# Routing and expert loads moved between two DMA queues in a fused attention and mixture-of-experts kernel

## The chip, the cores and the metric

One core of a Trainium2 chip runs the kernel. The metric is the device time of a run in microseconds (us). The core has five engines that run side by side, each through its own list of instructions in order: PE (matmuls), DVE (vector operations), ACT (activations, casts and copies), POOL (slow elementwise work, gathers) and SP (which only issues DMAs). DMAs are issued by SP, ACT or POOL and carried out by 16 shared DMA engines.

## The reference

Three layers follow each other. Attention: 2 batches, 8 heads, 576 positions, 64 wide; four heads see the last 32 positions, four see every 32nd position. Its result x is 1152 tokens of 512 numbers. A first mixture of 8 experts, of which each token uses one:

```
logits = x @ w_gate + modality_bias[modality_id]
e_idx = np.argmax(logits, axis=1)
...
for e in range(E):
    mask = e_idx == e
    h = np.maximum(x[mask] @ w1[e], 0.0)
    out[mask] = gate_w[mask, None] * (h @ w2[e])
```

And a second mixture of 4 experts, which every token uses, weighted by `domain_probs`. Each expert's first layer is 512 x 1024 and its second 1024 x 512, all in fp32.

## The kernel before

**Attention.** The 20 units of attention run in software steps s = 0 to 24 (L711 to L750): step s computes the scores of unit s (L307 to L341), the softmax of unit s and the result rows of unit s - 4 (`norm`, L350), the product with V of unit s - 3 (L398) and the transposes of the result of unit s - 5 (`xtr`, L425, PE line L430, into one PSUM bank that ACT copies out, L432 and L438). SP loads Q, K and V in pieces (`load_str`, `load_loc`, L197 to L223), small tables between the last of them (L237 to L245: constants, gate weights, bias, modalities, domain probabilities), and writes each unit's result rows to DRAM (L378, L383), from which tiles of tokens are gathered later.

**Routing.** `logits_part` (L442) multiplies transposed results with the gate weights (L450); `logits` (L458) transposes the sums (L466) and finds each token's expert; `ranks` (L511) and `lanes` (L524) number the tokens of each expert; L842 is the matmul that yields the list of tokens of every tile, `idx16`. The first batch is routed while the second is still in attention (`route0`, L668). Its favourite expert gets a tile of its own, the fill tile (`plain_tile`, L609: gather L596, transposes L617, first layer L623, transposes L636, second layer L643, scaled result L652), which runs in plain fp32 between the steps of the second batch's routing. SP reads the favourite from `gtab` (L165) and loads that expert's weights as eight blocks of 512 KB into `raws[0]` to `raws[7]`: two in `route0`, the rest in steps from 20 on. `EF` says how many pieces of the fill tile follow each step.

**Overflow tiles.** Behind the routing stands a nest of five branches on the number of tiles (L911), which is not entered. On its skip path SP waits until all transfers that it issued have landed; POOL does the same for its own.

**First mixture.** Eleven tiles of 128 tokens follow (`moe1`, L1005). Each fp32 operand is split into a high part (cast on ACT) and a rest (subtraction on DVE): `split`, L844, lines L846 and L847, for weights (`Weights.ahead`, at most `RING` = 10 blocks ahead), tokens (`x_parts`, transposes on PE L860) and hidden values (`htr`, L1032). The first layer is L1025, 24 matmuls for a tile; the second is L1046 to L1048. Weight blocks are loaded into the same eight `raws`, on the condition that the expert differs from that of the tile before. A transposed tile lies in one of two `ps_a` banks, which come free when the split is done.

**Second mixture.** 32 units of two blocks (L1257 to L1319, L1410 to L1430), not touched by the change.

The order on each engine is the order in which the program is written. Engines wait for each other by semaphores.

Of the kernel before, what the change touches and what calls it, by code (L numbers as in the profile page):

```python
# [18 lines left out]
ET = mybir.EngineType  # L19

P = 128
B, H, S, D = 2, 8, 576, 64
STRIDE = 32
P = 128
NTOK = B * S
DM = H * D
E1, E2 = 8, 4
FF = 1024
KC = DM // P
FC = FF // P  # L30
# [81 lines left out]
def fused_kernel(  # L112
# [42 lines left out]
    def w1_block(e, c):  # L155
        return w1a[bass.ds(e, 1), c * P : (c + 1) * P, :].rearrange("o p f -> p o f")

    def w2_block(e, u):
        return w2a[bass.ds(e, 1), u * 256 : (u + 1) * 256, :].rearrange("o (i p) f -> p (o i) f", p=P)

    def load_block(raw, src, cond=None):
        nc.sync.dma_start(out=raw.rearrange("p (c f) -> p c f", c=src.shape[1]), in_=src, cond=cond)

    def expert_value(ap):
        return nc.values_load(  # L165
            ap,
            engines=[ET.SP],
            min_val=0,
            max_val=E1 - 1,
            skip_runtime_bounds_check_because="clipped on chip",  # L170
        )
# [64 lines left out]
    load_str(3, (nc.gpsimd, nc.gpsimd))()  # L236
    nc.sync.dma_start(out=ct, in_=cst)  # L237
    wgs = ap.tile([P, KC, 32], F32, name="wgs")
    bsb = ap.tile([P, 2, E1], F32, name="bsb")
    mdi = ap.tile([P, NTT], I64, name="mdi")  # L240
    dps = ap.tile([P, NTT, E2], F32, name="dps")
    nc.sync.dma_start(out=wgs, in_=wg.rearrange("(c p) e -> p c e", p=P))
    nc.sync.dma_start(out=bsb, in_=bias.rearrange("(o m) e -> o m e", o=1).to_broadcast([P, 2, E1]))
    nc.sync.dma_start(out=mdi[:TQ], in_=mod)
    nc.sync.dma_start(out=dps[:TQ], in_=dp.rearrange("(j p) e -> p j e", p=TQ))  # L245
    load_loc(2, nc.gpsimd)

    mk16 = ap.tile([P, MW], BF16, name="mk16")
# [419 lines left out]
    def route0():  # L668
        logits_part(0, 1)
        logits_part(0, 0)  # L670
        yield from logits(0)
        rk = ranks(0)
        fav = favourite(rk[:, TPB])
        for _ in range(4):
            next(fav)
        eg.append(expert_value(gtab[0:1, 0:1]))
        for c in range(W1A):
            load_block(raws[c], w1_block(eg[0], c))
        yield
        for n, _ in enumerate(turns(lanes(0, rk), fav)):  # L680
            if n % 2:
                yield
        yield from first_tile()
# [22 lines left out]

    W1A, W1S = 2, 20
    nw = W1A
    r0 = route0()
    EF = 0, 0, 1, 1, 1, 2, 4  # L710
    for s in range(NU + 5):  # L711
# [20 lines left out]
        if s == 12:  # L732
            late_setup()
        if s == NU - 1:
            for t in range(NST + 1, NSX + 1):
                nc.sync.dma_start(out=ye[t * P : (t + 1) * P, :], in_=zero[:, :XW])
# [4 lines left out]
        if s == NU:  # L741
            for _ in r0:
                pass
            logits_part(1, 1)
        if s >= W1S and W1A <= nw < FC:
            for _ in range(2 if s==W1S else 1):
                load_block(raws[nw], w1_block(eg[0], nw) if nw < KC else w2_block(eg[0], nw - KC))
                nw += 1
        if s > NU:
            early(EF[s - NU - 1])  # L750
    while nw < FC:
        load_block(raws[nw], w2_block(eg[0], nw - KC))
        nw += 1
    logits_part(1, 0)
# [250 lines left out]
    def moe1(mp, tiles, W, gs, pool, mid, after, before_last):  # L1005
# [3 lines left out]
        def xprep(k):  # L1009
            g = gs.pop(k)  # L1010
            y = mp.tile([P, XW], F32, name="y", bufs=3)
            with_rows(y, idx16[:, tiles[k] : tiles[k] + 1])
            xs[k] = x_parts(g) if k else x0
            ys[k] = y
            if k + 2 < n:
                gs[k + 2] = m1_gather(tiles[k + 2], pool)
# [35 lines left out]
        xprep(1)  # L1052
        W.ahead()
        for k in range(n + 1):
# [6 lines left out]
            if k > 0:  # L1061
                htr(k - 1, 0, ht)
            W.ahead()
            if k == n:
# [3 lines left out]
            if k > 0:  # L1068
                htr(k - 1, 1, ht)
            W.ahead()  # L1070
            if k < n:
                mm1(k, ph, 2)
                if 0 < k < n - 1:
                    xprep(k + 1)
                W.ahead()
                mm1(k, ph, 3)
                h = mp.tile([P, FF], F32, name="h")
                for i in range(2):
                    nc.scalar.activation(h[:, 512 * i : 512 * (i + 1)], ph[i], AF.Relu)
                hs[k] = h  # L1080
                W.ahead()
# [292 lines left out]
    PC = Pieces()  # L1374
    W.ahead(3)
    x0 = x_parts(gs[0], x0)
    W.ahead(4)
    for _ in fill:
        pass
    W.owner[KC:] = [None] * (RAW - KC)  # L1380
    W.load()
    W.ahead()
    ectx.close()
# [114 lines left out]
def lay_out(inp):  # L1498
# [40 lines left out]
    for o, n in STRS:  # L1539
# [5 lines left out]
    vstr = with_one(vstr.reshape(2, 2, NCT, GQ, D).transpose(3, 1, 0, 2, 4))  # L1545
    w_gate = np.asarray(inp["moe_w_gate"])

    w1b = np.asarray(inp["moe2_w1"]).reshape(E2, 2, 2, P, 2, FC // 2, P)
# [8 lines left out]
        "mod": np.asarray(inp["moe_modality_id"]).reshape(NTT, TQ).T,  # L1557
        "wg": np.concatenate([w_gate, np.zeros((DM, 32 - E1), w_gate.dtype)], axis=1),
        "bias": inp["moe_modality_bias"],
        "w1a": inp["moe_w1"],  # L1560
        "w2a": inp["moe_w2"],
        "dp": inp["moe2_domain_probs"],
        "w1b": w1b.reshape(E2, FC // 2, P, -1),
# [33 lines left out]
```

## Time and profile before

| | |
|---|---|
| Median of 3 runs (lowest, highest) | 632.52 us (631.8, 635.23) |
| The profiled execution: time, and span in the profile | 631.46, 629.7 us |
| PE busy | 596.2 us, 95% of the span |
| DVE, ACT, POOL busy | 417.2 us (66%), 350.7 us (56%), 249.5 us (40%) |
| Moved by DMA | 79.14 MB, mean 126 GB/s |

The profile's times count from the start of the span, which lies 1.76 us inside the execution's own time. PE and PEld are the matmuls and the weight loads of the same engine. The attention ends near 66 us, the fill tile near 91, the first mixture near 240, and the second takes the rest.

### The profile page before, as it was taken

What the parts mean: (1) busy time and instruction counts of PE and PEld (TensorE: products, weight loads), DVE (VectorE), ACT (ScalarE), POOL (GpSimd) and SP (SyncE); (2) the same over time, 40 slices, a digit from 0 to 9 for tenths busy, and PEclk for the clock granted to TensorE, in tenths of its full rate; (3) what the DMA queues carried; (4) which work ended last, traced back from release to release, by engine and by line L of the source; (5) the groups of instructions that cost most, each with busy time, mean ns of one, the idle gap of its engine ahead of it and who ended that gap; (6) DMA issues with size and microseconds to landing.
All of it is one profiled execution on the core that took longest, in us unless ns stands there. A gap on an engine that the chain in (4) does not pass through costs nothing.

```text
span 629.7 us, 10388 instructions
## 1 busy us (share of the span) xinstructions
PE 596.2 (95%) x3620; PEld 498.8 (79%) x3620; DVE 417.2 (66%) x738; ACT 350.7 (56%) x690; POOL 249.5 (40%) x309
## 2 busy tenths in 40 slices
PE   4897798999999989999999999999999999999995
PEld 3554446888877878888988889898889988999984
DVE  3467369999896875668677677575565567557541
ACT  2354169888988874555656555554444544444420
POOL 9312023113696444275657656332342112312203
PEclk9999799999998999999999999999999999999999
DMA  8983951543479764353223231322421223121002
GB/s 189 200 187 109 315 161 47 168 143 94 144 229 316 231 222 150 122 165 101 101 92 110 72 129 68 135 84 88 144 87 67 69 74 124 71 68 68 0 2 84
DMA packets 35346, 79.14 MB, mean 126 GB/s; under 512 B 6520, under 2 KB 9856, under 8 KB 34904
## 3 DMA queue, kind: packets, MB, share of 16 engines
q1 hardware_dynamic: 30632, 67.08, 33.8%
q0 software_dynamic: 2784, 7.95, 4.1%
q10 hardware_dynamic: 1872, 3.39, 1.4%
q8 instruction: 30, 0.49, 0.3%
q14 instruction: 28, 0.23, 0.1%
HBM read 98.49 MB, written 9.28 MB: 171 GB/s over the span
## 4 chain that ended last, share of the span: by engine, by line
PE 77%; ACT 2%; DVE 2%; issue 2%; DMA 2%; POOL 1%; SPq 0%; POOLq 0%; DVEq 0%; ACTq 0%
PE ps_b L1269 9%; PE ps_b L1270 9%; PE ps_b L1271 9%; PE ps_b L1025 8%; PE ps_b L1418 7%; PE ps_b L1417 7%; PE ps_b L1420 7%; PE ps_a L1417 3%; PE ps_a L1418 3%; PE ps_a L1420 3%; PE ps_b L1048 3%; PE ps_b L1047 2%; PE ps_b L1046 2%; PE ps_a L1032 1%; ACT wh L846 1%
## 5 line engine op out<-in xcount | busy, mean ns | idle before, releaser
L1189 DVE TENSOR_TENSOR wl<-raw,wh 128x512 fp32r<-128x512 f32 (+1 forms) x160 | 125.6, 786 | 51.7 <-ACT wh L1188 51.0
L847 DVE TENSOR_TENSOR wl<-raw,wh 128x1024 fp32r<-128x1024 f32 x88 | 107.5, 1252 | 20.0 <-ACT wh L846 19.6
L1188 ACT CAST wh<-raw 128x512 fp32r<-128x512 f32 (+1 forms) x160 | 102.9, 664 | 3.5 <-POOL raw L1212 3.3
L1209 POOL TENSOR_TENSOR raw<-raw 128x256 f32<-128x256 f32 x32 | 24.1, 753 | 200.1 <-DVE wl L1189 200.1
L846 ACT CAST wh<-raw 128x1024 fp32r<-128x1024 f32 x88 | 90.1, 1055 | 8.6 <-ACT y L1092 3.6
L1281 DVE TENSOR_TENSOR m2t<-ps_b,raw 128x320 f32<-128x320 f32 (+1 forms) x93 | 42.1, 453 | 40.3 <-PE ps_b L1271 39.2
L1269 PE MATMUL ps_b<-xh,wh 128*128 128x256 f32 x224 | 63.8, 285 | 1.0 <-DVE xh L1281 0.5
L1271 PE MATMUL ps_b<-xh,wl 128*128 128x256 f32 x224 | 63.0, 281 | 0.0
L1270 PE MATMUL ps_b<-xl,wh 128*128 128x256 f32 x224 | 63.0, 281 | 0.0
L1269 PE MATMUL ps_b<-x,wh 128*128 128x320 f32 x160 | 49.6, 310 | 0.0
L1270 PE MATMUL ps_b<-x,wh 128*128 128x320 f32 x160 | 49.4, 309 | 0.0
L1271 PE MATMUL ps_b<-x,wl 128*128 128x320 f32 x160 | 49.4, 309 | 0.0
L1269 PEld LDWEIGHTS ps_b<-xh,wh 128*128 128x128 f32 x224 | 42.2, 189 | 7.1 <-ACT raw L1302 0.9
L1270 PEld LDWEIGHTS ps_b<-xl,wh 128*128 128x128 f32 x224 | 42.2, 188 | 4.2
L1284 ACT ACTIVATE hh2b<-m2t 128x256 fp32r<-128x256 f32 (+1 forms) x45 | 20.0, 443 | 44.3 <-DVE m2t L1281 41.0
L1284 ACT ACTIVATE hh2a<-m2t 128x256 fp32r<-128x256 f32 (+1 forms) x42 | 18.7, 445 | 44.5 <-DVE m2t L1281 44.5
L1271 PEld LDWEIGHTS ps_b<-xh,wl 128*128 128x128 f32 x224 | 42.3, 189 | 0.0
L605 POOL DMA_INDIRECT y<-xx,idx x11 | 12.9, 1177 | 60.4 <-DMA ye<-y 41.3
L1046 PE MATMUL ps_b<-wh,hh 128*128 128x512 f32 x88 | 35.1, 399 | 1.5 <-ACT hh L846 1.5
L1417 PE MATMUL ps_b<-wh,hh2a 128*128 128x512 f32 x90 | 35.5, 395 | 0.0
L1418 PE MATMUL ps_b<-wl,hh2a 128*128 128x512 f32 x90 | 35.5, 395 | 0.0
L1417 PE MATMUL ps_b<-wh,hh2b 128*128 128x512 f32 x90 | 35.5, 394 | 0.0
(274 smaller groups left out, 1546.0 us busy)
## 6 DMA issues: line engine op xcount, KB each, us to landing
raw<-in_w1a_dram SPq DMA_DIRECT2D x48, 512.0 KB
raw<-in_w2a_dram SPq DMA_DIRECT2D x48, 512.0 KB
raw<-in_w1b_dram SPq DMA_DIRECT2D x32, 512.0 KB
raw<-in_w2b_dram SPq DMA_DIRECT2D x32, 512.0 KB
ye<-y ACTq DMA_DIRECT2D x11, 260.0 KB
kvl<-in_kvl_dram SPq DMA_DIRECT2D x2, 792.0 KB
ye<-he SPq DMA_DIRECT2D x5, 260.0 KB
kvl<-in_kvl_dram SPq DMA_DIRECT2D x2, 614.0 KB
```

What stands on the lines that cost most here:

```text
L846: nc.scalar.copy(dst_h, src)
L847: nc.vector.tensor_tensor(dst_l, src, dst_h.bitcast(F32), op=ALU.subtract)
L1025: nc.tensor.matmul(ph[i], xx[:, s], ww[:, 512 * i : 512 * (i + 1)], start=first, stop=last)
L1046: nc.tensor.matmul(py, hh[:, s], wh[:, f], start=(kc == 0), stop=False)
L1188: return (lambda: nc.scalar.copy(h[:, s], src[:, s])), (lambda: nc.vector.tensor_tensor(l[:, s], src[:, s], h[:, s].bitcast(F32), op=ALU.s ...
L1189: lambda: nc.vector.tensor_tensor(l[:, s], src[:, s], h[:, s].bitcast(F32), op=ALU.subtract)
L1269: nc.tensor.matmul(ph, wh[:, kc], xh, start=first and kc == 0, stop=False, skip_group_check=True)
L1270: nc.tensor.matmul(ph, wh[:, kc], xl, start=False, stop=False, skip_group_check=True)
L1271: nc.tensor.matmul(ph, wl[:, kc], xh, start=False, stop=kc == 1, skip_group_check=True)
L1417: nc.tensor.matmul(po, hh, wh, start=(fb == 0 and fh == 1), stop=False, skip_group_check=part)
L1418: nc.tensor.matmul(po, hh, wl, start=False, stop=False, skip_group_check=part)
L1420: nc.tensor.matmul(po, hl, wh, start=False, stop=last, skip_group_check=part)
```

## The change

POOL instead of SP issues the tables, and all eight blocks of the fill expert's weights, in one run at step 20, when POOL has read the favourite for itself. Two tables are laid out on the host so that each partition's part is one run. SP writes the zero rows (an area that later gathers may touch) at step 14 instead of step 19. The fill tile's transposes come only after the logits of the second batch, and its first layer is shared out otherwise (`EF`). The second tile's tokens are split among the first weight splits instead of after ten of them, and most of the calls of `W.ahead` in the round of the first tile go. The lines of the changed program are 6 or 7 lower from `late_setup` on: L841 there is L847 here, L854 is L860, L1073 is L1079.

```
     load_str(3, (nc.gpsimd, nc.gpsimd))()
-    nc.sync.dma_start(out=ct, in_=cst)
...
-    nc.sync.dma_start(out=wgs, in_=wg.rearrange("(c p) e -> p c e", p=P))
-    nc.sync.dma_start(out=bsb, in_=bias.rearrange(...))
-    nc.sync.dma_start(out=mdi[:TQ], in_=mod)
-    nc.sync.dma_start(out=dps[:TQ], in_=dp.rearrange("(j p) e -> p j e", p=TQ))
     load_loc(2, nc.gpsimd)
+    nc.gpsimd.dma_start(out=ct, in_=cst)
+    nc.gpsimd.dma_start(out=wgs.rearrange("p c e -> p (c e)"), in_=wg)
+    nc.gpsimd.dma_start(out=bsb, in_=bias.rearrange(...))
+    nc.gpsimd.dma_start(out=mdi[:TQ], in_=mod)
+    nc.gpsimd.dma_start(out=dps[:TQ].rearrange("p j e -> p (j e)"), in_=dp)
...
         eg.append(expert_value(gtab[0:1, 0:1]))
-        for c in range(W1A):
-            load_block(raws[c], w1_block(eg[0], c))
...
-    W1A, W1S = 2, 20
-    nw = W1A
+    ZS = 14
-    EF = 0, 0, 1, 1, 1, 2, 4
+    EF = 0, 0, 0, 0, 0, 1, 3
...
-        if s == NU - 1:
+        if s == ZS:
             for t in range(NST + 1, NSX + 1):
                 nc.sync.dma_start(out=ye[t * P : (t + 1) * P, :], in_=zero[:, :XW])
...
-        if s >= W1S and W1A <= nw < FC:
-            for _ in range(2 if s==W1S else 1):
-                load_block(raws[nw], w1_block(eg[0], nw) if nw < KC else w2_block(eg[0], nw - KC))
-                nw += 1
+        if s == NU:
+            ep0 = expert_value(gtab[0:1, 0:1], ET.Pool)
+            for n in range(FC):
+                load_block(raws[n], w1_block(ep0, n) if n < KC else w2_block(ep0, n - KC), eng=nc.gpsimd)
...
         xprep(0)
         xprep(1)
-        W.ahead()
         for k in range(n + 1):
...
             if k > 0:
                 htr(k - 1, 0, ht)
-            W.ahead()
+                W.ahead()
...
             if k > 0:
                 htr(k - 1, 1, ht)
-            W.ahead()
+                W.ahead()
             if k < n:
                 mm1(k, ph, 2)
                 if 0 < k < n - 1:
                     xprep(k + 1)
-                W.ahead()
+                if k:
+                    W.ahead()
...
-    W.ahead(3)
-    x0 = x_parts(gs[0], x0)
-    W.ahead(4)
+    W.ahead(2)
+    x01 = [x_parts(gs[0], x0)]
+    W.ahead(KC + 1)
+    x01.append(x_parts(gs[1]))
+    W.ahead(KC + 2)
     for _ in fill:
         pass
     W.owner[KC:] = [None] * (RAW - KC)
     W.load()
-    W.ahead()
+    W.ahead(RING - 1)
```

POOL's order at the end of the attention, where the fill tile's gather (L596) and the gather of its routing rows (L605) stood next to each other (`raw_76` to `raw_83` are `raws[0]` to `raws[7]`; each ISA row works out a block's address):

```order
 L596 DMA g<-xe,idxe 128x512
+L165 TENSOR_LOAD gtab
+L162 ISA
+L162 DMA raw_76<-in_w1a_dram 128x1024
+L162 ISA
+L162 DMA raw_77<-in_w1a_dram 128x1024
+L162 ISA
+L162 DMA raw_78<-in_w1a_dram 128x1024
+L162 ISA
+L162 DMA raw_79<-in_w1a_dram 128x1024
+L162 ISA
+L162 DMA raw_80<-in_w2a_dram 128x2x512
```

Eight blocks (three more pairs of rows follow) now stand between L596 and L605, and ahead of the first tiles' gathers.

PE's order in the same place, from the last units' transposes to the ranks of the second batch (`ps_s` is the fill tile's first layer, `ps_m` logits and ranks):

```order
-L430 MATMUL ps_x<-mk,rw 128x128 x4
+L407 MATMUL ps_a<-kvl_157,pts 32x130 x8
+L430 MATMUL ps_x<-mk,rw 128x128 x6
+L450 MATMUL ps_m<-xtl,wgs 32x192 x6
 L617 MATMUL ps_t<-mk,g 128x128 x4
-L430 MATMUL ps_x<-mk,rw 128x128 x2
-L450 MATMUL ps_m<-xtl,wgs 32x192 x6
-L623 MATMUL ps_s<-raw_76,xte 128x512
 L466 MATMUL ps_m<-mk,lg 96x96 x2
-L623 MATMUL ps_s<-raw_76,xte 128x512
-L623 MATMUL ps_s<-raw_77,xte 128x512
+L623 MATMUL ps_s<-raw_76,xte 128x512 x2
```

The last transposes and the logits moved ahead of L617, and two of the eight matmuls of the fill tile's first layer instead of three now precede the ranks.

ACT's order in the round of the first tile, before (`h` is the first tile's hidden layer, `hh` its split, `xh` the second tile's tokens):

```order
L846 CAST wh<-raw_81 128x1024
L846 CAST xh<-ps_a 128x512
L846 CAST wh<-raw_82 128x1024
L846 CAST wh<-raw_83 128x1024
L846 CAST wh<-raw_76 128x1024
L1079 ACTIVATE h<-ps_b 128x512 x2
L846 CAST wh<-raw_77 128x1024
L846 CAST hh<-ps_a 128x512
```

And in the changed program:

```order
L840 CAST wh<-raw_80 128x1024
L1073 ACTIVATE h<-ps_b 128x512 x2
L840 CAST wh<-raw_81 128x1024
L840 CAST wh<-raw_82 128x1024
L840 CAST wh<-raw_83 128x1024
L840 CAST wh<-raw_76 128x1024
L840 CAST wh<-raw_77 128x1024
L840 CAST hh<-ps_a 128x512
```

Between `h` and `hh` stood one cast of weights, and now five; the second tile's `xh` moved up, ahead of the sixth weight cast. DVE's subtractions stand in the same order as these casts.

## Rows read from the trace of the kernel before

**Rows 1.** Windows: from and to, length, each engine's busy us, clock, DMA share, GB/s.
```profile
20.00:30.00 10.00, 7.88 (x95) 4.75 (x91) 4.16 (x16) 3.97 (x13) 1.51 (x3) 1.00 0.98 203
...
60.00:80.00 20.00, 15.43 (x108) 8.13 (x108) 8.81 (x55) 3.61 (x11) 2.73 (x3) 0.83 0.85 286
80.00:100.00 20.00, 17.58 (x75) 10.26 (x73) 14.05 (x21) 15.63 (x20) 9.30 (x8) 1.00 0.40 124
...
110.00:120.00 10.00, 10.00 (x52) 8.21 (x51) 9.28 (x10) 8.73 (x12) 2.18 (x2) 1.00 0.42 131
```

**Rows 2.** PE's timeline in the attention: start, us, instruction, idle before and releaser.
```profile
28.55 0.64 PE L323 MATMUL ps_s<-kvl,ql 128*32 128x128 f32 x16 [2.12 <-DMA ql<-in_qlo_dram]
...
49.20 0.64 PE L323 MATMUL ps_s<-kvl,ql 128*32 128x128 f32 x16 [1.03 <-DMA ql<-in_qlo_dram]
```

**Rows 3.** PE's timeline, fill tile and first tiles, and one later wait.
```profile
65.66 0.44 PE L430 MATMUL ps_x<-mk,rw 128*128 128x128 f32 x2 [0.46 <-ACT xtl L432]
68.86 1.12 PE L617 MATMUL ps_t<-mk,g 128*128 128x128 f32 x4 [2.76 <-DMA g<-xe,idxe]
...
70.33 2.08 PE L450 MATMUL ps_m<-xtl,wgs 128*32 128x192 f32 x12
...
74.21 0.52 PE L466 MATMUL ps_m<-mk,lg 96*96 96x96 f32 x2
...
76.66 4.54 PE L623 MATMUL ps_s<-raw,xte 128*128 128x512 f32 x10
81.03 0.45 PE L842 MATMUL ps_x<-boh,aoh 96*128 96x16 f16 x12
...
82.66 3.70 PE L643 MATMUL ps_a<-raw,hte 128*128 128x512 f32 x8
...
91.53 0.66 PE L860 MATMUL ps_a<-mk,g 128*128 128x128 f32 x4 [1.30 <-DVE xl L847]
91.94 0.71 PE L1025 MATMUL ps_b<-wh,xh 128*128 128x512 f32 x2
...
105.45 0.66 PE L860 MATMUL ps_a<-mk,g 128*128 128x128 f32 x4 [0.22 <-DVE hl L847]
...
107.33 0.40 PE L1046 MATMUL ps_b<-wh,hh 128*128 128x512 f32 x1
...
189.68 0.66 PE L1136 MATMUL ps_b<-mk,g 128*128 128x128 f32 x4 [2.29 <-DMA g<-ye,cidx]
```

**Rows 4.** Windows of 2 us, columns as in rows 1: clock, DMA share and rate.
```profile
68.00:70.00 2.00, 1.14 (x6) 1.14 (x6) 0.00 (x0) 0.00 (x0) 0.00 (x0) 0.50 0.87 319
...
78.00:80.00 2.00, 2.00 (x6) 0.95 (x5) 1.97 (x16) 0.00 (x0) 0.00 (x0) 1.00 1.05 390
...
192.00:194.00 2.00, 2.00 (x6) 1.54 (x5) 1.33 (x1) 1.55 (x3) 1.92 (x4) 0.50 1.04 386
```

**Rows 5.** ACT's timeline: the first weight casts, and the first hidden layer.
```profile
86.30 2.94 ACT L846 CAST wh<-raw 128x1024 fp32r<-128x1024 f32 x3 [3.13 <-SPq L911]
...
100.69 1.08 ACT L1079 ACTIVATE h<-ps_b 128x512 f32<-128x512 f32 x2
```

**Rows 6.** DVE's timeline: seven weight subtractions in a row, and the first of a hidden layer.
```profile
91.39 8.26 DVE L847 TENSOR_TENSOR wl<-raw,wh 128x1024 fp32r<-128x1024 f32 x7
...
104.71 0.68 DVE L847 TENSOR_TENSOR hl<-ps_a,hh 128x512 fp32r<-128x512 f32 x1
```

**Rows 7.** SP's timeline: the zero rows.
```profile
66.20 3.93 SPq L736 DMA_DIRECT2D ye<-he  x5
```

**Rows 8.** POOL's timeline: two gathers of 128 rows, as POOL issues them.
```profile
62.22 1.16 POOL L596 DMA_INDIRECT g<-xe,idxe  x1 [1.29 <-DVE rc L370]
...
95.10 1.97 POOL L852 DMA_INDIRECT g<-xe,idx  x1 [0.30 <-issue]
```

**Rows 9.** Source view of L852, the tiles' gathers: from issue to landing.
```profile
DMA to landing us min/median/max: 3.3/4.1/8.9
```

**Rows 10.** The chain that ended last: the first tile's first layer.
```profile
92.19 5.62 PE ps_b L1025 x24
```

More of the change, by code (lines that the diff above doesn't have):

```diff
@@ L159, in w2_block, with load_block, expert_value @@
         return w2a[bass.ds(e, 1), u * 256 : (u + 1) * 256, :].rearrange("o (i p) f -> p (o i) f", p=P)
-    def load_block(raw, src, cond=None):
-        nc.sync.dma_start(out=raw.rearrange("p (c f) -> p c f", c=src.shape[1]), in_=src, cond=cond)
-    def expert_value(ap):
+    def load_block(raw, src, cond=None, eng=nc.sync):
+        eng.dma_start(out=raw.rearrange("p (c f) -> p c f", c=src.shape[1]), in_=src, cond=cond)
+    def expert_value(ap, engine=ET.SP):
         return nc.values_load(
             ap,
-            engines=[ET.SP],
+            engines=[engine],
             min_val=0,
@@ L241, in fused_kernel @@
     dps = ap.tile([P, NTT, E2], F32, name="dps")
-    nc.sync.dma_start(out=wgs, in_=wg.rearrange("(c p) e -> p c e", p=P))
-    nc.sync.dma_start(out=bsb, in_=bias.rearrange("(o m) e -> o m e", o=1).to_broadcast([P, 2, E1]))
-    nc.sync.dma_start(out=mdi[:TQ], in_=mod)
-    nc.sync.dma_start(out=dps[:TQ], in_=dp.rearrange("(j p) e -> p j e", p=TQ))
     load_loc(2, nc.gpsimd)
+    nc.gpsimd.dma_start(out=ct, in_=cst)
+    nc.gpsimd.dma_start(out=wgs.rearrange("p c e -> p (c e)"), in_=wg)
+    nc.gpsimd.dma_start(out=bsb, in_=bias.rearrange("(o m) e -> o m e", o=1).to_broadcast([P, 2, E1]))
+    nc.gpsimd.dma_start(out=mdi[:TQ], in_=mod)
+    nc.gpsimd.dma_start(out=dps[:TQ].rearrange("p j e -> p (j e)"), in_=dp)
     mk16 = ap.tile([P, MW], BF16, name="mk16")
@@ L744, in fused_kernel @@
             logits_part(1, 1)
-        if s >= W1S and W1A <= nw < FC:
-            for _ in range(2 if s==W1S else 1):
-                load_block(raws[nw], w1_block(eg[0], nw) if nw < KC else w2_block(eg[0], nw - KC))
-                nw += 1
+        if s == NU:
+            ep0 = expert_value(gtab[0:1, 0:1], ET.Pool)
+            for n in range(FC):
+                load_block(raws[n], w1_block(ep0, n) if n < KC else w2_block(ep0, n - KC), eng=nc.gpsimd)
         if s > NU:
             early(EF[s - NU - 1])
-    while nw < FC:
-        load_block(raws[nw], w2_block(eg[0], nw - KC))
-        nw += 1
     logits_part(1, 0)
@@ L1012, in xprep @@
             with_rows(y, idx16[:, tiles[k] : tiles[k] + 1])
-            xs[k] = x_parts(g) if k else x0
+            xs[k] = x_parts(g) if k > 1 else x01[k]
             ys[k] = y
@@ L1546, in lay_out @@
     w_gate = np.asarray(inp["moe_w_gate"])
+    w_gate = np.concatenate([w_gate, np.zeros((DM, 32 - E1), w_gate.dtype)], axis=1)
     w1b = np.asarray(inp["moe2_w1"]).reshape(E2, 2, 2, P, 2, FC // 2, P)
@@ L1557, in lay_out @@
         "mod": np.asarray(inp["moe_modality_id"]).reshape(NTT, TQ).T,
-        "wg": np.concatenate([w_gate, np.zeros((DM, 32 - E1), w_gate.dtype)], axis=1),
+        "wg": w_gate.reshape(KC, P, 32).transpose(1, 0, 2).reshape(P, -1),
         "bias": inp["moe_modality_bias"],
@@ L1561, in lay_out @@
         "w2a": inp["moe_w2"],
-        "dp": inp["moe2_domain_probs"],
+        "dp": np.asarray(inp["moe2_domain_probs"]).reshape(NTT, TQ, E2).transpose(1, 0, 2).reshape(TQ, -1),
         "w1b": w1b.reshape(E2, FC // 2, P, -1),
```

## Prediction

> **What bounds the kernel now.** I read the stages by windows first. From 110 us on PE is busy 10.00 of 10 us, while from 60 to 100 us it has holes, 15.43 and 17.58 us busy of 20 [rows 1]. So what the start-up loses or wins is handed on to the end nearly one to one. Then PE's own timeline of the attention, whose last wait for data is 1.03 us before L323 at 49.20 [rows 2]; then that of the fill tile and of the first tiles, the stretch that the change is about [rows 3]: L617 waits 2.76 us for the fill tile's gather, logits (L450, L466) stand behind it in PE's order, L842 gives the token list of every tile at 81.03, the first tile's product L1025 starts at 91.94, and its second layer L1046 at 107.33. The clock rows beside it show 0.50, the lower of the two levels (1.2 of 2.4 GHz), after that wait [rows 4]. ACT's rows show what held the first weight split: 3.13 us on SP at L911 [rows 5], the branch at which SP waits until all its transfers have landed, among them the fill expert's. The reader should see that three things stand in a row here, late logits, a late L911 and DVE splitting without a gap (7 splits in 8.26 us [rows 6]), and that removing one hands the wait to the next.
>
> **Tables and tokens loads (attention).** SP no longer stops at five small loads, so the last pieces are asked for earlier and the 1.03 us before L323 goes [rows 2]. Against it the tables, about 0.26 MB by their shapes, now run on POOL's queue beside the pieces that L323 awaits at 28.55; at 203 GB/s [rows 1] they may add 1.3 us to that wait. Ends: -1.0 and +0.3. I take **-0.5**, nearer the gain, because the stall that goes is in a row and the other one is only possible. What POOL does behind them, memsets for the routing, is waited for only some ten units later; the five issues cost nothing there.
>
> **Zeros.** Five writes, 3.93 us of SP [rows 7], leave the place ahead of the last four result rows and go to step 14. There they stand before the rows of later units, which only the tile gathers read at about 78. I cost that at nothing; if the cover goes (SP still behind at step 20), it is at most the same 3.93 us on those rows, and then the first gather is late.
>
> **Logits ahead of L617.** In the new order PE does the last L430 after 65.66 as soon as ACT has freed its one bank (it waited 0.46 us for that at 65.66 too), and L450 another 0.9 us behind it, near 67.3. At 70.33 L450 takes 2.08 us at the lower clock; I take half, 1.0, for the full one [rows 3]. That ends it at 68.3. The gather for L617, issued at 62.22 [rows 8], landed for 68.86 with zeros and two weight blocks beside it; the median of its kin is 4.1 us [rows 9], so it is no longer the later one. I allow 1.4 us for L617 (1.12) and its copy on ACT, so L623 starts at 69.7, with the attention's 0.5 at 69.2. Its 16 records at 4.54/10 = 0.45 us [rows 3] and the ranks between them, for which I allow 0.5, end at 76.9: L842 at 77.0 instead of 81.03, **-4.0**. DVE's routing between L466 and L842 runs under L623, as it does now.
>
> **The fill expert's weights on POOL.** POOL issues L596, reads the expert, for which I allow 0.5, and then issues eight blocks, from 62.9 + 0.5 = 63.4 (the attention's 0.5 taken off). No row shows such a transfer on POOL. The nearest are its gathers of 128 rows: 1.16 us at 62.22, 1.97 at 95.10 [rows 8]. The second-layer blocks have 256 runs, so I double them. At 1.16 the eight take 4 x 1.16 + 4 x 2.32 = 13.9 us, until 77.3; then the fill tile's row gather that was moved behind them (wanted only at 86, no cost) until 78.5, where the first tile's gather is due (77.9). I take 1.16, as DVE is busy 8.81 of 20 us there and 14.05 of 20 around 95.10 [rows 1]; the other end is a rival below. Bytes: 4.2 MB at 390 GB/s [rows 4] are 10.8 us, down by 76; at 319, by 78. L643 wants its first block at 77.0 + 1.6 = 78.6. It fits, barely.
>
> **What SP gains.** With rows only on its queue SP passes L911 once the last of them has landed, ahead of need. ACT then splits as soon as the fill tile's own copies are done, 4 us earlier than now; it and DVE are no longer the last to arrive.
>
> **First tile.** L643's first half 78.6 to 82.2 (3.70 for eight records [rows 3]); gather down at 77.9 + 4.1 = 82.0; transposes to 82.8; second half to 86.4; second tile's transposes, which no longer wait 1.30 for DVE, to 86.9. So L1025 starts at 86.9, not 91.94: **-5.0**, the 0.5 included.
>
> **The early split of the second tile.** Both orders put fourteen weight splits and two token splits ahead of DVE's first hl. But now five of them, all the casts between h and hh on ACT, come after h, where there was one. From L1025's start: its 24 matmuls 5.62 [rows 10], h 1.08 [rows 5], one cast 2.94/3 = 0.98, five subtractions at 8.26/7 = 1.18, hl 0.6 [rows 6], then the third tile's transposes, which need hl's bank, and the last product, 107.33 - 105.45 = 1.9 [rows 3]: 16.1 us to L1046 against 15.4 now, **+0.7**. PE itself needs only about 10.7 of the 14.2 us to hl, so it idles 3.5 us in one piece.
>
> **The clock after that.** Idle of 2.29 us at 189.68 [rows 3] and of 2.76 at 68.86 each put PE on 0.50 [rows 4]. 3.4 us at half speed lose 1.7. Ends: 0 and 1.7. I take **+1.6**, since both nearest idle times are shorter than 3.5.
>
> **Sum.** -5.0 + 0.7 + 1.6 = -2.7. The profiled execution took 631.46, so 628.8; the median of the runs is 1.06 above it, which I carry along: **629.8**, or -0.43%.
>
> **Rivals.** *B, PE is fed.* The hole is shorter or the clock holds, and the attention gives its full 1.0: -5.5 + 0.7 = -4.8, 627.7. For it: the 3.5 are a difference of two sums, and each of the five splits that takes 0.2 less shortens it. Against: it would have to fall well under 2.29 to be sure of the clock.
>
> *C, hidden anyway.* L617's wait shrinks, but PE is so thinly used between 60 and 68 that the clock falls as before; then 3.4 us at half speed cost 1.7 of the 5.0, and the order costs stay: -3.3 + 0.7 + 1.6 = -1.0, 631.5. For it: 0.50 at 68 to 70 [rows 4]. Against: L430, L450 and L617 now follow each other. The Trainium skill, "DMA: Bandwidth & Descriptors", section on issuing engines, says that transfers from all issuers share the same engines and that spreading them saves only issue time. The trace agrees as to the engines (share 1.05 while the fill expert's blocks land [rows 4]); taken alone, that rule leaves this part of the change worth nothing, 632.5.
>
> *D, slower: POOL becomes the bound.* At 1.97 for 128 rows and 3.94 for 256 the eight blocks last until 63.4 + 23.6 = 87.0, the row gather until 89.0; the first tile's gather lands at 93.1, half of L643 and the transposes follow, L1025 at 97.8: +5.9 + 0.7 + 1.6 = +8.2, 640.7. It decides from the point where L1025 comes no earlier than 89.6, the gather issued at 80.8, so nine transfers at 1.9 us each. For it: 1.97 exists [rows 8]. Against: it stands between splits of DVE [rows 6]. The Trainium skill, "SBUF — State Buffer", section on the two sides, warns that POOL cannot write descriptors while DVE holds their shared port, and counsels to issue from SP or ACT. The trace agrees as far as the two rows go (1.97 amid splits, 1.16 without); by that rule D would need DVE at large operands while POOL issues, which it is not before its first split.
>
> **How the numbers follow.** Forecast 0.57, B 0.20, C 0.13, D 0.10. About 0.5% (3.2 us) is what a measurement here can tell from no change. The forecast's own range is 627.5 to 632 (attention -1.0 to +0.3, start of L1025 by 1.2 either way); about a third of it, 0.21, lies below 629.4. Faster: 0.20 + 0.21 = 0.41. Slower: D, 0.10. Same: 0.49. The range 625.5 to 633.5 takes in B with a start of L1025 still 2 us earlier, and C with 2 us of scatter; it leaves out D.
>
> **What would show it.** L323's second wait gone; L466 near 69, before the first L623; L842 at 77; POOL's eight issues at about 1.2 and 2.3 us each, ended by 78; ACT's first wh no longer behind L911; L1025 near 87; on PE a hole of 3 to 4 us before the third tile's transposes, with 0.50 behind it; L1046 near 103, then no other difference. It is wrong if the issues last near 2 us or more, if 0.50 shows at 68 to 72 again, or if L1046 is not 16 us behind L1025.

## The result, and the profile after

| | before | changed |
|---|---|---|
| Median of 18 runs (lowest, highest) | 631.91 us (630.06, 635.23) | 635.83 us (633.68, 638.89) |
| Ratio, 95% interval | | 1.0065 (1.0046 to 1.0084) |
| The profiled execution, its span | 631.46, 629.7 us | 638.43, 636.8 us |
| Granted clock of the profiled execution | 0.987 | 0.976 |

The change costs about 4.1 us, 0.65%. The forecast was 629.8 us, and 635.83 lies above its range. The profiled execution is one of the longer ones of the changed kernel, so it shows more than the median: 7 us.

PE's timeline of the changed program (start, us, instruction, idle before and what ended it), the places of [rows 2] and [rows 3]:

```profile
21.28 0.65 PE L323 MATMUL ps_s<-kvl,ql 128*32 128x128 f32 x16 [2.08 <-DMA ql<-in_qlo_dram]
...
29.82 1.08 PE L323 MATMUL ps_s<-kvl,ql 128*32 128x128 f32 x16 [3.00 <-DMA ql<-in_qlo_dram]
...
69.98 1.37 PE L450 MATMUL ps_m<-xtl,wgs 128*32 128x192 f32 x12
71.28 0.66 PE L617 MATMUL ps_t<-mk,g 128*128 128x128 f32 x4
71.77 0.35 PE L466 MATMUL ps_m<-mk,lg 96*96 96x96 f32 x2
...
80.00 0.45 PE L836 MATMUL ps_x<-boh,aoh 96*128 96x16 f16 x12
...
81.62 3.70 PE L643 MATMUL ps_a<-raw,hte 128*128 128x512 f32 x8
88.08 1.12 PE L854 MATMUL ps_a<-mk,g 128*128 128x128 f32 x4 [2.75 <-DMA g<-xe,idx]
...
94.25 0.71 PE L1019 MATMUL ps_b<-wh,xh 128*128 128x512 f32 x2
...
108.75 1.11 PE L854 MATMUL ps_a<-mk,g 128*128 128x128 f32 x4 [3.55 <-DVE hl L841]
...
112.22 0.63 PE L1040 MATMUL ps_b<-wh,hh 128*128 128x512 f32 x1
```

L617's wait of 2.76 us and the one before L323 at 49.20 are gone, and L466 comes at 71.77 instead of 74.21, though the attention ended later here. But L836 (L842 of before) hands over its token list only 1 us earlier, the second half of L643 stands behind a wait for the first tile's gather, and L1019 (L1025) starts 2.3 us later instead of 5.0 earlier. L1040 (L1046) is 18.0 us behind it instead of 15.4, with a hole of 3.55 us in one piece ahead of the third tile's transposes.

Windows of the same execution, columns as in [rows 1]:

```profile
30.00:40.00 10.00, 10.00 (x129) 5.96 (x124) 4.99 (x18) 4.07 (x13) 0.94 (x5) 0.68 1.04 196
60.00:80.00 20.00, 16.96 (x129) 8.59 (x130) 11.68 (x69) 5.69 (x17) 6.68 (x10) 0.91 0.80 286
80.00:100.00 20.00, 16.84 (x70) 10.31 (x69) 10.72 (x13) 12.21 (x15) 8.67 (x8) 0.91 0.34 91
110.00:120.00 10.00, 10.00 (x35) 7.89 (x34) 8.10 (x8) 7.30 (x9) 0.00 (x0) 0.76 0.00 1
```

The clock gained in 60:80 (0.91, before 0.83: L617's wait and the fall behind it are gone) and lost in 20:40 and from 80 to 120: 0.68 in 30:40 (before 0.83), 0.91 in 80:100 and 0.76 in 110:120, where both were 1.00. While PE waits in 80:100, the DMA engines move 91 GB/s, where 390 was measured at 78 to 80 before [rows 4]: they wait as well.

What they wait for stands in POOL's timeline:

```profile
64.82 0.61 POOL L162 DMA_DIRECT2D raw<-in_w1a_dram  x1
65.77 1.71 POOL L162 DMA_DIRECT2D raw<-in_w1a_dram  x3 [0.33 <-issue]
67.61 2.17 POOL L162 DMA_DIRECT2D raw<-in_w2a_dram  x3
82.28 0.72 POOL L162 DMA_DIRECT2D raw<-in_w2a_dram  x1 [12.51 <-SPq L905]
...
84.62 0.99 POOL L846 DMA_INDIRECT g<-xe,idx  x1 [0.30 <-issue]
```

Seven blocks are issued in 5 us (0.53 to 0.74 us each). The eighth waits 12.5 us, and behind it, on an engine that works in order, stands the first tile's gather, 84.62 instead of 82.02, although its list was there at 80.7. In the program's order the eighth block waits for the writes of the result rows of units 12 to 15: they are kept in `raws[7]`, the buffer it loads into. SP's timeline (rows of units 14 and 15, then of the last four):

```profile
65.93 4.77 SPq L383 DMA_DIRECT2D xe<-raw  x4
70.81 6.13 SPq L378 DMA_DIRECT2D xe<-rw  x4
```

And DVE's, the list itself:

```profile
80.49 0.17 DVE L837 CAST idx<-ps_x 128x16 int32<-128x16 f32 x1 [0.22 <-PE ps_x L836]
```

The DMA view of two stretches, by queue (packets, MB, share of the 16 engines; q0 is POOL's, q1 SP's), from 68 to 76 us:

```profile
q0 software_dynamic: 819, 2.97, 97.2%
q1 hardware_dynamic: 186, 0.08, 3.4%
```

and from 76 to 82 us:

```profile
q1 hardware_dynamic: 1243, 0.70, 39.0%
q0 software_dynamic: 128, 0.44, 18.7%
```

SP issued these rows from 65.93 on. While the seven blocks came in, 8 us long, rows got 3.4% of the engines, 38 or 39 packets in each 2 us from 70 to 76; in the 2 us after, as the blocks ran out, 341. So POOL's burst delayed the very writes that its own last block, and then the gathers of all tiles, had to wait for.

### The profile page after: what moved, and what is told of

It reads as the page before. It is cut to its first block, busy times and chain, and to the rows that moved or that the text cites. A ratio compares the mean times of both kernels' runs of the same rounds, so it can differ in the third digit from the quotient of the medians.

```text
span 636.8 us, 10397 instructions
## 1 busy us (share of the span) xinstructions
PE 599.0 (94%) x3620; PEld 501.3 (79%) x3620; DVE 418.0 (66%) x738; ACT 351.8 (55%) x690; POOL 257.6 (40%) x322
## 4 chain that ended last, share of the span: by engine, by line
PE 75%; DMA 3%; DVE 2%; ACT 2%; issue 2%; POOL 1%; POOLq 0%; ACTq 0%; DVEq 0%
PE ps_b L1263 9%; PE ps_b L1264 9%; PE ps_b L1265 9%; PE ps_b L1019 7%; PE ps_b L1414 7%; PE ps_b L1413 7%; PE ps_b L1416 7%; PE ps_a L1413 3%; PE ps_a L1414 3%; PE ps_a L1416 3%; PE ps_b L1042 3%; PE ps_b L1041 2%; PE ps_b L1040 2%; DVE wl L841 1%; PE ps_a L1026 1%
## 5 line engine op out<-in xcount | busy, mean ns | idle before, releaser
L841 DVE TENSOR_TENSOR wl<-raw,wh 128x1024 fp32r<-128x1024 f32 x88 | 108.0, 1252 | 23.7 <-ACT wh L840 22.4
L605 POOL DMA_INDIRECT y<-xx,idx x11 | 13.1, 1192 | 64.2 <-ACT wh L840 21.9
L1040 PE MATMUL ps_b<-wh,hh 128*128 128x512 f32 x88 | 35.7, 406 | 1.5 <-ACT hh L840 1.5
L1042 PE MATMUL ps_b<-wh,hl 128*128 128x512 f32 x88 | 35.6, 405 | 0.1
```

Of the source, the lines that this page charges most:

```text
L841: nc.vector.tensor_tensor(dst_l, src, dst_h.bitcast(F32), op=ALU.subtract)
L1040: nc.tensor.matmul(py, hh[:, s], wh[:, f], start=(kc == 0), stop=False)
L1042: nc.tensor.matmul(py, hl[:, s], wh[:, f], start=False, stop=(kc == FC - 1))
```

## The experiments

Ratios are to runs of the kernel before on the same chip, with 95% intervals. The parts of the change are called tables, burst (the eight blocks on POOL), zeros, logits (`EF`) and order (of the splits). Diffs start from the changed kernel unless the text says otherwise. The capital letters are the theories and rivals that each expectation names; T, in most of them, is that the burst holds back SP's result rows, that gathers wait for these, and that the order of the splits costs time of its own.

**Tables back on SP.**

```
-    nc.gpsimd.dma_start(out=ct, in_=cst)
+    nc.sync.dma_start(out=ct, in_=cst)
...
```

> The changed kernel with the five tables issued by SP again, between the same two pieces as before; all else as changed. Theory T (three separate losses: tables in the attention, the burst of weights on POOL's queue, the order of the splits): the wait for ql near 28.5 is about 2.1 us again instead of 3.0, the one at 21 goes, the clock falls once less before 40 us, the last result transposes and logits stand about 3 us earlier (L450 of the second half near 67 instead of 69.98). Of these 3 us the first tile keeps 1.5 to 3, because the result rows still have to land: about 633.5 us against 635.8. Rival V (tables of 0.26 MB are too small to matter, the lower clock in the attention is chance): within 1 us of the changed kernel.

1.0058 (1.0034 to 1.0082): within 1 us of the changed kernel, as rival V said. L323 still waited 1.61 and 3.79 us for `ql`. In all twenty profiles, whatever the tables' queue, that wait near 29 us lies between 1.99 and 4.68 us; the wait and the clock behind it scatter from profile to profile.

**Blocks back on SP**, between the result rows, as before.

```
-            for n in range(FC):
-                load_block(raws[n], w1_block(ep0, n) if ..., eng=nc.gpsimd)
+        if s >= W1S and W1A <= nw < FC:
+            ...
+                load_block(raws[nw], w1_block(eg[0], nw) if ...)
```

> The changed kernel with the fill expert's eight blocks issued by SP between the result rows, in the places of before; tables, zeros, order of logits and splits as changed. Theory T (the burst of eight blocks fills the DMA engines, the result rows on SP's queue land late, and both the eighth block and the first tile's gather wait for them): POOL's wait of 12.5 us is gone, the gather is issued near 81, about 3.5 us earlier, L1019 stands near 92 instead of 94.25: about 633.5 us. Rival U (POOL's issuing is good and only the shared buffer of the eighth block is at fault): blocks come later than from POOL, the first layer of the fill tile or its second half waits for them, and the time stays within 1 us of 635.8.

1.0011 (0.999 to 1.0032): 3.4 us of the 4.1 are gone, as theory T said. POOL and PE of this run (lines are 7 higher):

```profile
81.09 0.95 POOL L853 DMA_INDIRECT g<-xe,idx  x1 [11.70 <-DMA raw<-in_w2a_dram]
```

```profile
89.29 0.71 PE L1026 MATMUL ps_b<-wh,xh 128*128 128x512 f32 x2
...
103.78 0.66 PE L861 MATMUL ps_a<-mk,g 128*128 128x128 f32 x4 [3.55 <-DVE hl L848]
```

The first tile starts 2.65 us earlier than in the kernel before; the hole behind it is as long as in the changed kernel. The list came at 78.86, as L623 waited 0.70 and 1.98 us for blocks, and the gather went out only 1.6 us after `idx` was there (79.5), by the trace behind a transfer of SP.

**Rows of units 12 to 15 in buffers of their own.**

```
-    EARLY = 16
+    EARLY = 12
...
-            rw = a3.tile([P, 4, D], F32, name="rw", bufs=5) if v >= EARLY else early_rows(v)
+            rw = a3.tile([P, 4, D], F32, name="rw", bufs=9) if v >= EARLY else early_rows(v)
```

> The changed kernel with the rows of units 12 to 15 kept in four more buffers of their own instead of the eighth weight buffer, so that the eighth block no longer waits until they are written out. Rival U (POOL stood still only because of that buffer): all eight issued by 70.5, second half of L643 directly behind the first, first gather at 80.6 right behind the token list, L1019 near 90: about 631.5 us. Theory T (the rows themselves land late because the burst holds the DMA engines): the eighth block goes out at 70, but the rows are written no earlier, the gather waits for them until 82 to 83.5, L1019 92 to 93: about 634 us.

1.0066 (1.0043 to 1.0088): no gain at all, against rival U and against T's own 634. POOL and PE:

```profile
65.55 2.87 POOL L162 DMA_DIRECT2D raw<-in_w2a_dram  x4
...
83.43 0.99 POOL L846 DMA_INDIRECT g<-xe,idx  x1 [5.83 <-SPq L905]
```

```profile
76.69 0.45 PE L836 MATMUL ps_x<-boh,aoh 96*128 96x16 f16 x12
```

The eighth block goes out with the others and the list is there at 77, but the gather stands 5.83 us for the rows. The shared buffer was only one of two things that waited for them.

**Old order of the splits.**

```
-    W.ahead(2)
-    x01 = [x_parts(gs[0], x0)]
-    W.ahead(KC + 1)
-    x01.append(x_parts(gs[1]))
-    W.ahead(KC + 2)
+    W.ahead(3)
+    x0 = x_parts(gs[0], x0)
+    W.ahead(4)
...
```

> The changed kernel with the old order of the splits (three weight blocks, first tile's tokens, one block, then the rest; the second tile's tokens behind them; the old places of the calls in the first tile's round). Theory T: L1040 follows L1019 by 15.4 us instead of 18.0, the hole of 3.55 us ahead of the third tile's transposes and the low clock behind it go: about 633.2 us. Rival W (the hole comes from ACT and DVE starting the first tile late, as they waited for the fill tile and the gather, not from their order): a hole of 3 us or more stays somewhere between L1019 and L1040, and the time stays within 1 us of 635.8.

1.0042 (1.0021 to 1.0063), 1.5 us less. PE:

```profile
108.94 0.66 PE L854 MATMUL ps_a<-mk,g 128*128 128x128 f32 x4 [0.27 <-DVE hl L841]
...
110.82 0.40 PE L1040 MATMUL ps_b<-wh,hh 128*128 128x512 f32 x1
```

L1040 is 16.15 us behind L1019 (94.67), the hole is gone, PE waits 0.91 and 1.16 us for the second tile's parts instead, and the clock holds, as T said, though with 1.5 of its 2.6 us.

**Blocks and order back** (both diffs).

> The changed kernel with both the eight blocks on SP between the rows and the old order of the splits; what is left of the change is the tables on POOL, the zeros at step 14 and the logits ahead of L617. If the two losses stand apart (theory T): the first tile starts near 89.5 as in the run with the blocks on SP alone, L1040's counterpart follows 16 us later instead of 17.1, and 632.7 less 1.2 gives about 631.5 us, level with the kernel before. If the order of the splits only mattered because the gather was late (W): no better than 632.7.

0.9987 (0.9967 to 1.0006). Taken out of the changed kernel, the two parts add up: without the burst the order costs 1.5 us again, without the order the burst 3.5. Tables, zeros and logits together are worth what is left, 0.8 us, which the interval does not tell from nothing.

**The burst alone**: tables, zeros, logits and order as before.

> The kernel before with the burst alone: POOL issues the fill expert's eight blocks in one run at step 20; tables (in the new layout) on SP, zeros at step 19, logits and splits in the old order. Theory T (the burst holds back the result rows on SP's queue, and the gathers wait for these): gather of the first tile at 83 or later instead of 82.0, the fill tile's second half behind it, first tile near 94 to 95; as the same part cost 3.4 us in the changed kernel, about 634.5 us. Rival Z (the burst hurts only together with the early logits, as before the token list came no earlier than 81 anyway): within 1 us of 631.

1.0073 (1.0049 to 1.0098), 4.6 us: as T said, and more than expected. Five writes of zeros still stand among the last rows, and zeros and rows are both late. PE, POOL, and the queues from 66 to 78 us:

```profile
83.70 1.97 PE L636 MATMUL ps_t<-mk,he 128*128 128x128 f32 x8 [5.63 <-ACT he L631]
```

```profile
85.60 0.98 POOL L846 DMA_INDIRECT g<-xe,idx  x1 [6.68 <-SPq L905]
```

```profile
q0 software_dynamic: 903, 3.30, 77.5%
q1 hardware_dynamic: 583, 1.02, 22.2%
```

The zeros are read from the buffer that L631 writes next. On ACT, L631 stood 10.38 us, by the trace until a later write of SP's (`xx`) had landed, and L636 behind it; that the zeros were what it waited for is argued from the program.

**Logits alone**, on the kernel before:

```
-    EF = 0, 0, 1, 1, 1, 2, 4
+    EF = 0, 0, 0, 0, 0, 1, 3
```

> The kernel before with the logits ahead of L617 as the one change (the line EF). Theory T: the token list comes near 79 instead of 81, held a little by the first-layer blocks behind the zeros on SP; first tile near 90, about 630 us. Rival X (C of the prediction: the fill tile's blocks and the result rows land when they did, so that the earlier logits change no gather): first tile at 91 to 92 and 631 to 632 us.

1.0006 (0.999 to 1.0023): no change, as rival X said. L617's wait is gone and L466 comes at 70.61, but L623 then waits 2.39 us for its second pair of blocks and the list comes at 81.49, as before.

**Order alone**, on the kernel before with the tables in the new layout.

> The kernel before with the changed order of the splits as its one part (and the tables in the new layout). If the order costs what the first two pairs gave: a hole of about 3.3 us ahead of the third tile's transposes, second layer 17 to 17.5 us behind the first tile's start, 1.4 to 1.7 us slower, about 632.7 us. If it costs more wherever the first tile is not held by something else: 635 to 636 us, as in the third pair.

1.0049 (1.0028 to 1.007), 3.1 us, between the two:

```profile
106.06 0.70 PE L861 MATMUL ps_a<-mk,g 128*128 128x128 f32 x4 [3.61 <-DVE hl L848]
...
109.12 0.63 PE L1047 MATMUL ps_b<-wh,hh 128*128 128x512 f32 x1
```

The same hole with all else as before, and the second layer 17.6 us behind the first tile's start (91.49).

Put into the kernel before one at a time, burst (4.6), order (3.1) and logits (0.4) come to 8.1 us, about twice the 4.1 us of the whole change. So the parts add up when they are taken out of the changed kernel, and not when they are put in; for the burst the late zeros are a likely reason, for the order it stays open.

**Half the burst**, with the old order: POOL issues four blocks, SP the other four.

```
+            for n in range(KC):
+                load_block(raws[n], w1_block(ep0, n), eng=nc.gpsimd)
+        for n in {NU + 1: (0,), NU + 2: (1,), NU + 3: (2, 3)}.get(s, ()):
+            load_block(raws[KC + n], w2_block(eg[0], n))
```

> The changed kernel with the old order of the splits, and with the burst halved: POOL issues only the four first-layer blocks, SP the four second-layer blocks behind the last result rows. Theory T (the size of the burst beside the rows decides): no wait of POOL for a buffer, rows down by about 77, token list at 77, gather issued by 79, first tile near 88: about 629.5 us. Rival Y (any block of weights on POOL's queue holds SP's rows back, and SP's later blocks with them): gather at 82 or later, L643 waits for its blocks, 633 us or more.

0.9995 (0.9975 to 1.0015). List at 78.08, but the gather goes out only at 80.97, 5.94 us of wait before it: between T and rival Y. With the zeros on POOL as well:

> As the kernel with four blocks on POOL, and the five writes of zeros issued by POOL at step 12 instead of SP at step 14. If SP's backlog of 2.9 us there still held the last rows: rows and second-layer blocks 2 to 3 us earlier, up to 1 us better than that kernel. If the rows wait for the DMA engines and not for SP: the same within 0.7 us, or worse by up to 1 us where the 1.3 MB of zeros delay the last pieces of Q and K that L323 waits for near 49.

1.0004 (0.9978 to 1.0031), the same: SP's backlog of 2.9 us was not what held the rows.

**Rows ahead of the second-layer blocks**, all on SP, old order: four blocks as soon as the expert is known, the last rows, then four blocks.

> Zeros at step 14, tables on POOL, logits ahead of L617, old order of the splits; SP issues all four first-layer blocks as soon as it knows the expert, then the last result rows, and the four second-layer blocks only behind the last row. Theory T: L623 no longer waits for a block (1.85 us with the blocks between the rows), token list at 77 to 78, rows down by 75 to 77, gather issued at 79, first tile near 88.5: about 628 us. Rival Q (2.1 MB on SP's own queue ahead of the rows hold them as the burst on POOL's did, since a transfer of SP can only go out when the one eight places earlier has landed): gather at 82 or later, 630 us or more.

0.9988 (0.9969 to 1.0007). POOL and PE:

```profile
78.99 0.95 POOL L849 DMA_INDIRECT g<-xe,idx  x1 [9.20 <-SPq L908]
```

```profile
84.43 0.66 PE L857 MATMUL ps_a<-mk,g 128*128 128x128 f32 x4 [1.24 <-DMA g<-xe,idx]
```

The gather is issued at 79 as T had it, but lands 5.4 us later, in the middle of the four blocks; what one wait gave back the next took. With more buffers for the rows, and then with the four first blocks on POOL:

> The same, and the rows of units 12 to 15 kept in four more buffers, so that the last second-layer block does not wait until they have landed. If that wait stands on the path: L643's second half up to 2 us earlier and up to 1 us better than the same kernel without. If the first tile's gather decides (the rows): the same within 0.7 us.

> As the last, but the four first-layer blocks are issued by POOL at step 20 instead of SP. Theory T: the rows keep SP's queue to themselves until the last one, second-layer blocks follow; gather issued by 79, first tile near 88: 628 us. If any block on POOL's queue outruns the rows (the half burst gave 630.7 with the second-layer blocks between the rows): gather at 81 again and 630 to 631 us.

0.9993 (0.9974 to 1.0012) and 0.9991 (0.9973 to 1.0008): the same as without.

**Rows of units 11 to 16 on POOL**, which computes them, ahead of its own burst (those of 14 to 16 behind the fill tile's gather).

```
+            if 11 <= v < 14:
+                write_row(v, rwf, nc.gpsimd)
+            elif 14 <= v < NU - PT:
+                late_rows.append((v, rwf))
+            else:
+                write_row(v, rwf, nc.sync)
```

> The changed kernel, in which POOL issues the result rows of units 11 to 16 too (it computes them), those of 14 to 16 behind the fill tile's gather and ahead of the burst; SP keeps the rows of units 17 to 19. Theory T1 (rows on SP's queue lose to the burst on the DMA engines): rows of 11 to 16 land before the burst, the eighth block no longer waits 12.5 us, only three late rows are left behind the burst; gather near 80, about 3 us off: 633 us. Theory T2 (SP's backlog, not the engines, made the rows late): as SP has nothing else to do, the last three rows go out at 67 to 69 and land at once, gather at 78 to 79, first tile near 90: 631 to 632 us. Neither (the bytes as such): gather at 82 again, 635 us.

1.0057 (1.0035 to 1.0078). POOL and PE:

```profile
84.34 0.99 POOL L859 DMA_INDIRECT g<-xe,idx  x1 [9.82 <-DVE idx L850]
```

```profile
73.38 3.75 PE L634 MATMUL ps_s<-raw,xte 128*128 128x512 f32 x4 [3.57 <-DMA raw<-in_w1a_dram]
```

The eighth block no longer waits, and for the first time the gather follows its list directly: the rows were down. Neither T1's nor T2's time came, since the blocks now stand behind the rows on POOL, the fill tile's first layer waits 3.57 us for them, and the clock falls there. As SP's last rows were also issued ahead of the burst here, T1 and T2 are not told apart by this run; the shares of the queues above speak for T1.

> The same with the old order of the splits: 1.4 us less than the run before it, as the order of the splits cost in both pairs of runs so far.

1.0037 (1.0015 to 1.006), 1.3 us less, as expected.

**Rows of units 11 to 16 on POOL, blocks on SP**, old order.

> Rows of units 11 to 16 on POOL, and all eight weight blocks on SP (four as soon as the expert is known, four behind the last row), zeros at step 14, logits first, old order of the splits. If the early token list is worth what the prediction gave it once rows and blocks are down in time: list at 77, gather at 78 and landed by 82, first tile at 87 to 88, 627 us. If the DMA engines are full in this stretch whatever the order (the kernel with the second-layer blocks last had its gather out at 79 and landed only at 84.4): first tile at 89 to 91 again, 630 us.

0.9975 (0.9955 to 0.9995), median 629.96 us: faster than both kernels, though by less than the expected 627. POOL and PE:

```profile
77.49 0.99 POOL L862 DMA_INDIRECT g<-xe,idx  x1 [10.19 <-DVE idx L853]
```

```profile
76.55 0.45 PE L852 MATMUL ps_x<-boh,aoh 96*128 96x16 f16 x12
...
86.94 0.71 PE L1035 MATMUL ps_b<-wh,xh 128*128 128x512 f32 x2
...
102.54 0.40 PE L1056 MATMUL ps_b<-wh,hh 128*128 128x512 f32 x1
```

Here the prediction's times stand: list 76.55 (77.0 forecast), gather 77.49 (77.9), first tile 86.94 (86.9). This profiled execution took 625.91 us at a clock of 0.995, the shortest of the twelve; the others have clocks of 0.986 to 0.994.

**The same with the changed order.**

> The kernel with the rows of units 11 to 16 on POOL and the eight blocks on SP, now with the changed order of the splits; so everything of the change but the burst, and the late rows out of the way. If the prediction's last two terms hold: the first tile starts near 86.9, the second layer follows 17 us behind (15.6 with the old order), a hole of 3.3 us or more ahead of the third tile's transposes and the low clock behind it: 1.5 to 2.3 us more than with the old order, 631.5 to 632.3 us by the median. Rival B (an early start feeds PE, the hole closes): within 0.7 us of 630.

1.0063 (1.0041 to 1.0085). The hole is there (3.25 us), and the second layer 17.5 us behind; but 5.5 us more than with the old order is three times what the first two pairs gave. Part of it lies ahead of the splits in these two profiles: here the list came at 80.53 and the first tile started at 90.41, 3.5 us later than with the old order.

**Early tokens, old calls**: the second tile's split early, one cast instead of five behind `h`.

> The kernel with rows on POOL and blocks on SP, second tile's tokens split early as in the change, but the calls in the first tile's round in their old places, so that one cast and not five stands between h and hh. If the five casts are at fault (the prediction's reason): second layer 15.6 us behind, no hole over 1.5 us, 629.5 to 630.2 us. If not their place but the early tokens are (PE runs through the second tile's half and then stands in one piece until DVE, which has the same sixteen subtractions to do in any order, reaches hl): a hole of 2.5 us or more with the low clock behind it stays, 631 us or more.

1.0006 (0.9981 to 1.003). The second layer is 15.7 us behind (108.00 after 92.34) and nothing waits ahead of the third tile's transposes, so the five casts are at fault for that hole. Another wait opens ahead of the first hidden layer's transposes:

```profile
102.44 0.66 PE L1042 MATMUL ps_a<-mk,h 128*128 128x128 f32 x4 [2.82 <-ACT h L1089]
```

But the clock stays at 1.00 behind it, and the distance is the 15.6 us of the old order, so in this profile the round of the first tile lost nothing. The tile itself came 5.4 us later than with the old order, because L628 (L617 of before) waited 2.88 us for the fill tile's gather again, at 0.50 from 71 to 77, and the list came at 82.46. The 2 us by which this kernel's runs lie above the old order's are thus not explained, and the two intervals overlap.

## Why the prediction was wrong

- **The fill expert's weights on POOL** is the step that failed first, and about half of the 6.8 us between the forecast change (-2.7) and the measured one (+4.1). It counted what POOL needs to issue eight blocks, "until 77.3", and had that far too dear: 0.53 to 0.74 us each against 1.16 and 2.32. It did not ask what each block's buffer holds (the eighth waits for rows), nor what seven blocks of 512 KB in a row do to SP's writes beside them. Cost: 3.4 us in the changed kernel, 4.6 alone. Rival D had the right sign and place, POOL as the bound, by a mechanism that did not occur: issuing was not slow. The Trainium skill, "SBUF — State Buffer", section on the two sides, warns of POOL's descriptor writing beside DVE. The issues at 64.82 to 69.8 show nothing of it, but DVE was busy for only 1.53 of these 5 us, so they hardly test it.
- **Zeros.** "Costed at nothing", as the rows of later units are read only at about 78: the zeros were not at fault, but the same sentence took the rows for granted, and they are what landed late, near 82.
- **First tile**, 86.9, follows in part from that step: 94.25 measured, and still 89.29 with the burst undone, since on SP's queue too the blocks and rows were not down when the list came. The sum had no wait for either, and that is the term it put at nothing. With both down in time, and the old order, it came at 86.94, in the shortest of twelve executions.
- **Logits ahead of L617**, 77.0: right as far as its own terms go. Lists came at 76.55 to 78.08 in the seven profiles with this order in which neither the attention nor the first-layer blocks were late; in the profile of the changed kernel at 80.00, as the attention ended later. It was worth nothing by itself (1.0006): hidden anyway, as rival C said, though by blocks, rows and gather and not by the clock. In the other nine profiles with this order the list came at 78.55 to 83.40.
- **Attention**, -0.5: the wait at 49.20 went, as said, another at 21.28 came; the tables' queue made no difference that can be measured, and with the tables back on SP the wait at 49.20 was gone too.
- **What SP gains.** SP no longer waits for these blocks at L905, but the rows that it still waits for were late: it issued its next load at 83.97, and ACT's first weight cast came at 84.08 instead of 86.30: 2.2 us of the forecast 4.
- **The early split**, +0.7, and **the clock after that**, +1.6: right in kind. The hole was to be 3.5 us and is 3.55, with the lower clock behind it (windows, 110:120). The size is not settled. L1046 was to stand 16.1 us behind L1025, and another distance was named as a sign of being wrong; it stood 17.1 to 18.0 us behind in the seven profiles with this hole, as part of the lower clock falls ahead of it. The 3.4 us at the lower clock is what the trace of the kernel before shows behind 189.68; behind 68.86 it is about 6.8. Behind the hole it was about 3.4 us in five of the seven profiles and 6.8 in two, the changed kernel's among them, where half speed took some 3 us and not 1.6. Together 2.3 forecast; measured 1.5, 1.5, 1.3 and 3.1 us in four comparisons, 5.5 in a fifth.
- **The sum without the failed step.** With the burst undone the kernel was still 0.7 us slower than before (1.0011). With the rows down in time as well, and the changed order kept, it was 4.0 us slower (1.0063, six runs), where the forecast has -2.7. So undoing the failed step does not bring the forecast back, and the runs do not show every term that is missing.

What stays open: the fifth comparison; the scatter of `ql`'s wait, which let the last matmul of the first batch's routing (L587) start at 60.80 in one of its two profiles and 63.44 in the other, with the same attention; and whether rows lose to the burst by the engines' way of taking turns alone. The Trainium skill, "DMA: Bandwidth & Descriptors", section on queues, rings and completion order, has each engine take turns between queues a whole packet at a time; 97.2% against 3.4% agrees with turns of unequal size only in part: the packets differ 8-fold in size (3.6 and 0.43 KB on average) but also 4-fold in number (819 and 186), and no run shows what a turn holds.

## What to carry to other kernels

A transfer moved to another queue still shares the 16 engines (97.2% and 3.4% of them here). Before a burst is moved, list the small writes under way beside it and who waits for them, and what the burst's own buffers are still read for; here rows first, then blocks, was worth 0.7% against the burst (1.0042 to 0.9975 with the same order of the splits). An issuer that works in order is blocked by whichever of its transfers has to wait (12.51 us here), so a block that may wait does not belong ahead of a gather. And casts or subtractions that one engine must do anyway should not be piled up where PE then stands in one piece: the clock fell behind each such hole of 3.25 to 3.61 us here.

## What the runs showed of the hardware

In the changed kernel direct transfers of 512 KB cost POOL 0.53 to 0.61 us to issue with 128 runs and 0.71 to 0.74 with 256, less than a gather of 128 rows (0.95 to 1.97). From 68 to 76 us, writes in runs of 1 KB on SP's queue got 3.4% of the engines beside blocks in runs of 4 and 2 KB on POOL's.

Idle of 2.29 and 2.76 us (kernel before) was followed by a granted clock of 0.50, and 2.82 us ahead of L1042 (early tokens, old calls) was not: the clock was 1.00 from 102 to 116 us.

In the kernel before, the five tables on SP went out one by one, waiting for earlier loads of `ql`, `kvl`, `kvl`, `ql` and `kqs`: in each case SP's own transfer of eight places earlier.

Much of each difference is clock. Span times one minus the granted clock, an upper bound of what the lower clock took, is 8.2 us in the mean over 35 runs of the kernel before and 11.2 over 18 of the changed one, 3 of the 4.9 us by which their mean spans differ (these 35 were taken beside the first experiments; the pairs of the table give 4.1); it is 10.4 with the order alone, 11.0 with the burst alone, and 6.1 in the fastest kernel.
